# Attention and two expert layers on one core: the weights of the first layer converted in 16 pieces of 1024 columns instead of 32 of 512, with a new order of the first 32 steps

## The chip, the cores and the metric

The kernel runs on one core of a Trainium2 chip. A core has five engines with their own instruction queues, each worked off in order: PE (matrix products into PSUM), DVE (elementwise work and reductions), ACT (activation functions and copies), POOL (elementwise work on SBUF only, and indirect DMAs) and SP, which here issues the other DMAs. The metric is the device time of one execution in microseconds, as a median of runs.

## What is computed

```python
attn = chunked_attention(q, k, v)          # 8 batches, 8 heads, 576 tokens in chunks of 64, head_dim 64
x = attn as (4608 tokens, 512)
h = x @ w_in                               # (512, 2048)
g = max(h, 0) + alpha * min(h, 0)
x = g @ w_out                              # (2048, 512)
e = argmax(x @ w_gate)                     # 8 experts
out[token] = gate(token) * (max(x @ w1[e], 0) @ w2[e])
```

`w_in` and `w_out` come as float64; everything else is float32. Every product is made of three float32r products of a high and a low part of each operand (high x high, high x low, low x high).

## The kernel before

The tokens lie as 36 tiles of 128 rows in 18 batches j of two tiles. A *step* is one pair (j, m): `mm1` (X in the order below) makes 128 of the 2048 columns of h for a batch's 256 tokens, 12 matmuls of 256 columns; `mm2` (Y) multiplies them into the batch's two output tiles, 6 matmuls of 512 columns. There are 288 steps. Batches 0 and 1 are interleaved over the first 32 steps, group of columns by group (four groups g of 4 m): steps 0 to 3 are batch 0 with group 0, 4 to 7 batch 1 with group 0, 8 to 11 batch 0 with group 1, and so on. So group g's weights are wanted only from step 8 g on. From step 32 a loop runs over the steps; attention for later batches, gating, and the splitting of the expert weights (`eload`, `esplit`, written back to DRAM as `wsp`) are hung on step numbers. After step 287 come the experts, tile by tile, with their weights loaded into the same ring buffer (`load_early`, `refill`).

The first 32 steps are written out by hand as `ORDER`, a list of tokens, letter and number, worked off at build time; it sets the order within each engine's queue. The letters, with the line of the instruction in the profile:

- DMAs on SP: I piece of the weights (L481), Q and K q and k (L165, L167, L173, L174), V v (L178), N alpha.
- The conversion of piece k, from float64 words to a high and a low float32r part: v (ACT, L486) and s, u, m (DVE, L490, L495, L499) put together a float32 from the two 32-bit words; h (ACT, L502) rounds it to the high part; l (L506, on POOL with suffix G, on DVE with V) subtracts for the low part. v, s and u read the raw words, and the last of them frees their buffer.
- A step: X (PE, L331), r (ACT, L346) and x (DVE, L351, g_x in the code) apply alpha, f (ACT, L355) and g (L359, on POOL with G, on DVE with V; g_l in the code) split the result, Y (PE, L381). The PSUM banks for h alternate between two, and x is the last that reads one.
- Attention for tile i: S (PE, scores, L189), A, B (DVE, L202, L211), E (ACT, L218), C (DVE, three instructions, L223 to L225), D (L230, POOL or DVE), T (PE, L239), P (ACT, L245), O (PE, L302), H (ACT, L314) and L (DVE, L318) split it for mm1. A batch's X wants both its tiles' L.
- W warm-up matmuls (L914), p and b what else is hung on a step's number (gating from step 30, `load_wgb` and `fill_rows` at 24, the first `eload` at 25).

A piece is 128 rows by 512 columns of w_in (one quarter of the contracted dimension of a group) or 512 columns of w_out (one m). X of group 0 adds up over all four pieces 0 to 3; Y of m wants piece 4 + m. Raw words have four buffers (`sg_raw`), the float32 three (`sg_m`, later those of `eload` and of the expert rows `load`), u two (`sg_u`). The ring is two tiles; groups 0 and 2 lie in the first, 1 and 3 in the second:

```python
W_in = [ring[0][:, 0], ring[2][:, 0], ring[0][:, 1], ring[2][:, 1]]
W_out = [ring[1][:, 0], ring[3][:, 0], ring[1][:, 1], ring[3][:, 1]]
```

In the last 16 steps `load_early(0, c)`, c from 0 to 3, loads the first expert's weights over groups that are no longer needed, at steps 4, 7, 8 and 11 of the 16; `load_early(1, c)` follows in `START`, the written-out beginning of the experts' stage, where `m1` and `m2` are the two products.

Of the kernel before, what the change touches and what calls it, by code (L numbers as in the profile page):

```python
# [18 lines left out]
ORDER = """  # L19
I0 Q0 Q1 I1 N0 V0 I2 I3 Z0 W12 S0 S1 K1 s0V u0 A0 W10 B0 v0 E0 m0 I4 A1 C0 D0G s1V B1 T0 h0 E1 W6 v1 P0 u1 s2V C1 m1  # L20
I5 D1G l0G O0 T1 s3V u2 v2 P1 h1 l1G H0 v3 O1 S2 u3 m2 V1 I6 H1 h2 l2G S3 L0 m3 L1 A2 h3 v4 l3G I7 s4V B2 A3 E2 B3
p0 X0 r0 C2 x0 D2G b0 p1 E3 X1 f0 r1 v5 C3 u4 s5V m4 I8 x1 D3G g0G T2 v6 P2 h4 l4G b1 p2 X2 r2 T3 O2 u5 s6V m5 x2 u6
s7V I9 K2 P3 f1 h5 f2 m6 I10 b2 p3 g1V g2G l5G O3 X3 Y0 v7 H2 H3 h6 r3 v8 u7 L3 s8V x3 L2 u8 m7 I11 b3 p4 f3 h7 l6V
g3G s9V Y1 X4 r4 m8 x4 l7G b4 p5 h8 v9 X5 u9 I12 r5 f4 v10 l8G I13 s10V m9 x5 u10 s11V h9 u11 g4G m10 I14 V2 b5 Y2
p6 v11 f5 g5G l9G X6 r6 h10 l10G I15 m11 s12V x6 u12 s13V h11 v12 l11G m12 I16 b6 p7 Y3 X7 S4 r7 u13 x7 v13 h12 f6
l12G g6G I17 v14 s14V m13 u14 h13 l13G m14 I18 b7 Y4 p8 v15 f7 h14 g7G X8 Y5 s15V s16V u15 r8 l14G u16 x8 m15 I19 f8
v16 b8 p9 Y6 X9 r9 h15 A4 m16 g8G l15G I20 s17V v17 h16 l16G B4 u17 x9 I21 f9 b9 p10 g9G Y7 X10 r10 m17 s18V s19V
x10 u18 h17 E4 v18 v19 l17G b10 p11 f10 X11 r11 C4 I22 m18 u19 x11 D4G g10G v20 h18 l18G b11 S5 Y8 p12 f11 g11G Y9
X12 r12 s20V m19 I23 u20 x12 h19 l19G m20 I24 s21V f12 v21 h20 b12 p13 g12V l20G T4 X13 Y10 v22 P4 r13 u21 s22V u22
I25 m21 x13 h21 m22 I26 s23V u23 b13 p14 f13 g13G l21G X14 h22 r14 v23 s24V x14 l22G b14 Y11 p15 f14 g14G X15 Y12  # L30
r15 v24 u24 A5 x15 m23 I27 I28 v25 b15 p16 f15 h23 g15V l23G X16 Y13 r16 s25V m24 u25 B5 x16 v26 h24 f16 E5 b16 p17
g16G l24V X17 Y14 r17 s26V m25 x17 u26 C5 I29 f17 h25 s27V m26 I30 b17 p18 v27 l25G g17G X18 Y15 r18 x18 s28V u27
h26 v28 I31 b18 p19 f18 l26G g18G X19 Y16 r19 u28 m27 x19 v29 h27 b19 p20 f19 l27V D5V X20 v30 r20 s29V u29 m28 x20
m29 g19V s30V u30 b20 Y17 p21 h28 f20 l28G g20G Y18 X21 r21 h29 l29V x21 s31V m30 u31 b21 p22 f21 g21G X22 O4 T5 Y19
h30 r22 P5 v31 x22 m31 h31 f22 g22G l30V b22 p23 X23 r23 x23 b23 Y20 p24 f23 g23G l31G Y21 X24 r24 x24 b24 p25 f24 g24G
X25 Y22 r25 x25 b25 p26 f25 g25G X26 Y23 r26 x26 b26 Y24 p27 f26 X27 r27 x27 g26V b27 Y25 p28 f27 g27V X28 Y26 H4
r28 x28 b28 p29 f28 g28V X29 O5 r29 L4 x29 f29 H5 b29 Y27 p30 g29G X30 r30 L5 x30 b30 p31 Y28 X31 r31 f30 x31 b31
Y29 g30G
"""
# [3 lines left out]
def tile_attention_moe(ctx, tc, q, k, v, w_in, w_out, alpha, w_gate, w1, w2, out):  # L43
    nc = tc.nc
    NB = q.shape[0]
# [18 lines left out]

    duo = [ring_p.tile([128, 2, 2, 2, 4, 512], F32R, name=f"ring{c}") for c in range(2)]
    ring = [duo[c // 2][:, :, c % 2] for c in range(4)]
    W_in = [ring[0][:, 0], ring[2][:, 0], ring[0][:, 1], ring[2][:, 1]]
    W_out = [ring[1][:, 0], ring[3][:, 0], ring[1][:, 1], ring[3][:, 1]]

# [414 lines left out]
    def conv_v(k):
        im[k] = sg_m([128, 512], "m")
        nc.scalar.activation(out=im[k], in_=iraw[k][:, :, 1].bitcast(F32), func=ACTF.Abs, scale=2.0 ** -112)  # L486

    def conv_s(k, eng=nc.vector):
        iu[k] = sg_u([128, 512], "u", I32)
        eng.tensor_scalar(out=iu[k], in0=iraw[k][:, :, 0], scalar1=29, scalar2=None, op0=ALU.logical_shift_right)  # L490
# [535 lines left out]
```

## Time and profile before

| | us |
|---|---|
| median of 3 runs | 1364.6 (1363.75 to 1366.65) |
| the profiled execution | 1365.83 |
| its span, first to last instruction | 1364.1 |
| PE busy | 1319.9 (97%) |
| DVE busy | 998.6 (73%) |
| ACT busy | 740.8 (54%) |
| POOL busy | 725.1 (53%) |

Mean granted TensorE clock 0.99. PE is busy nearly throughout; in the page's 40 slices of 34 us its first four are at 7, 7, 8 and 8 tenths, and nearly all the others are full. DVE's first five are at 7, 9, 9, 6 and 6 tenths. The share over the whole span says little here, since the stages have different limits.

### The profile page before, as it was taken

To read this page: it belongs to the slowest core of one execution; us is meant where nothing else is said; L and a number is where in the kernel's file an instruction comes from. 1 tells how busy PE (TensorE), PEld (TensorE's weight loads), DVE (VectorE), ACT (ScalarE), POOL (GpSimd) and SP (SyncE) were. 2 spreads that over 40 slices of the span, in tenths; PEclk is the share of its full clock that TensorE was granted. 3 is DMA by queue.
4 is the path that set the end of the run, shared out by engine and by line. 5 is a ranking of instruction groups with operands and counts; after the bars stand their busy time and mean duration, and the time that the engine had idled before them with its cause. 6 is when DMAs were issued, how large, how long until landed. Compare 5 with 4: busy or idle time off the path is not lost. (4 is left out here: it accounts for less than half of the span.)

```text
span 1364.1 us, 29980 instructions
## 1 busy us (share of the span) xinstructions
PE 1319.9 (97%) x9515; PEld 1152.2 (84%) x9515; DVE 998.6 (73%) x2524; ACT 740.8 (54%) x1993; POOL 725.1 (53%) x754
## 2 busy tenths in 40 slices
PE   7788999999999999999999999999999999999997
PEld 6577899999999999999999999887788888888885
DVE  7996687788787878877877887558976556666553
ACT  4454544555555555555546455339666666656663
POOL 4563244676766656666665765343444444444442
PEclk9989999999999999999999999999999999999999
DMA  6655213666565666656666662194124526966660
GB/s 235 200 163 177 85 32 109 216 200 219 197 219 197 216 210 209 223 184 210 215 212 218 196 229 88 40 365 185 46 71 171 173 58 227 348 202 257 199 269 34
DMA packets 107105, 249.08 MB, mean 183 GB/s; under 512 B 15360, under 2 KB 36352, under 8 KB 102848
## 3 DMA queue, kind: packets, MB, share of 16 engines
q1 hardware_dynamic: 100944, 227.37, 49.7%
q0 software_dynamic: 6000, 19.70, 3.8%
q8 instruction: 84, 1.38, 0.4%
q14 instruction: 77, 0.63, 0.1%
HBM read 401.39 MB, written 88.91 MB: 359 GB/s over the span
## 5 line engine op out<-in xcount | busy, mean ns | idle before, releaser
L331 PEld LDWEIGHTS h<-xt,ring 128*128 128x128 f32 x3456 | 455.7, 193 | 44.2 <-DVE r L351 17.0
L331 PE MATMUL h<-xt,ring 128*128 128x256 f32 x3456 | 465.8, 285 | 16.8 <-DVE r L351 13.1
L381 PE MATMUL y<-ring,g 128*128 128x512 f32 x1728 | 453.7, 398 | 3.1 <-POOL g L359 2.1
L381 PEld LDWEIGHTS y<-ring,g 128*128 128x128 f32 x1728 | 306.3, 189 | 58.3 <-POOL g L359 3.0
L359 POOL TENSOR_TENSOR g<-r,g 128x256 fp32r<-128x256 f32 x281 | 237.6, 847 | 166.2 <-ACT g L355 146.0
L351 DVE SCALAR_TENSOR_TENSOR r<-r,calpha,h 128x256 f32<-128x256 f32 x288 | 137.0, 476 | 173.7 <-ACT r L346 173.1
L405 DVE CUSTOM_DVE_ANT_0 junk<-row,wgb 128x512 bf16<-128x512 f32 x288 | 257.5, 894 | 8.1 <-ACT row L393 3.8
L469 POOL TENSOR_TENSOR sp<-eraw,sp 128x512 fp32r<-128x512 f32 x128 | 179.3, 1401 | 107.0 <-ACT sp L468 99.1
L697 DVE TENSOR_SCALAR hx<-h 32x128 f32<-32x128 f32 x576 | 165.3, 287 | 89.9 <-PE h L679 82.4
L679 PE MATMUL y<-ring,hT 128*128 (+1 forms) x936 | 221.7, 392 | 4.8 <-POOL hT L667 2.6
L346 ACT ACTIVATE r<-h 128x256 f32<-128x256 f32 x288 | 110.1, 382 | 209.2 <-PE h L331 147.7
L679 PE MATMUL h<-ring,xT 128*128 (+1 forms) x936 | 219.1, 389 | 1.7 <-DMA ring<-wsp 1.7
L667 POOL TENSOR_TENSOR hT<-z,hT 128x512 fp32r<-128x512 f32 x78 | 100.7, 1309 | 220.7 <-ACT hT L666 219.5
L679 PEld LDWEIGHTS y<-ring,hT 128*128 128x128 f32 x936 | 176.1, 189 | 44.0 <-POOL hT L667 4.3
L679 PEld LDWEIGHTS h<-ring,xT 128*128 128x128 f32 x936 | 175.5, 188 | 38.4 <-issue 2.1
L355 ACT ACTIVATE g<-r 128x256 fp32r<-128x256 f32 x288 | 119.5, 415 | 147.6 <-PE y L381 106.3
L695 ACT ACTIVATE hx<-h 32x128 f32<-32x128 f32 x672 | 179.5, 267 | 10.3 <-PE h L679 2.8
L666 ACT ACTIVATE hT<-z 128x512 fp32r<-128x512 f32 x78 | 48.0, 633 | 115.4 <-DVE z L664 111.1
L260 ACT ACTIVATE px<-s 32x256 f32<-32x256 f32 x240 | 89.6, 374 | 3.1 <-DVE s L249 0.3
L468 ACT ACTIVATE sp<-eraw 128x512 fp32r<-128x512 f32 x128 | 80.5, 629 | 2.8 <-DMA wsp<-sp 2.1
L664 DVE STREAM_TRANSPOSE z<-xg 128x512 f32<-128x512 f32 x39 | 27.6, 707 | 47.5 <-POOL hT L667 47.4
L667 POOL TENSOR_TENSOR xT<-z,xT 128x512 fp32r<-128x512 f32 x39 | 51.7, 1326 | 16.1 <-ACT xT L666 15.5
(163 smaller groups left out, 958.3 us busy)
## 6 DMA issues: line engine op xcount, KB each, us to landing
ring<-wsp SPq DMA_DIRECT2D x70, 4096.0 KB
wsp<-sp SPq DMA_DIRECT2D x128, 512.0 KB
eraw<-in_w SPq DMA_DIRECT2D x128, 256.0 KB
ring<-wsp SPq DMA_DIRECT2D x8, 2048.0 KB
xg<-xs SPq DMA_DIRECT2D x156, 64.0 KB
vt<-in_v SPq DMA_DIRECT2D x18, 512.0 KB
qt<-in_q SPq DMA_DIRECT2D x17, 512.0 KB
kt<-in_k SPq DMA_DIRECT2D x17, 512.0 KB
```

The costliest lines, as they stand in the source:

```text
L331: nc.tensor.matmul(out=h, lhsT=w[:, wl, a, 128 * mi:128 * mi + 128], rhs=x[:, xl, a], start=(n == 0), stop=(n == 11),)
L346: nc.scalar.activation(out=r, in_=h, func=ACTF.Relu, scale=-1.0)
L351: nc.vector.scalar_tensor_tensor(out=r, in0=r, scalar=calpha[:, m:m + 1], in1=h, op0=ALU.mult, op1=ALU.add)
L355: nc.scalar.activation(out=gs[j, m][:, 0], in_=rs[j, m][0], func=ACTF.Copy)
L359: eng.tensor_tensor(out=g[:, 1], in0=r, in1=g[:, 0].bitcast(F32), op=ALU.subtract)
L381: nc.tensor.matmul(out=ys[j][t], lhsT=g[:, gl, 128 * t:128 * t + 128], rhs=w[:, wl, mi], start=(m == 0 and n == 0), stop=(m == MF - 1 and ...
L405: nc.vector.tensor_tensor_reduce(out=junk, in0=r[:, 0:512], in1=wgb[e // 2][:, e % 2], scale=1.0, scalar=0.0, op0=ALU.mult, op1=ALU.add, a ...
L469: eng.tensor_tensor(out=dst[:, 1], in0=raw, in1=dst[:, 0].bitcast(F32), op=ALU.subtract)
L667: nc.gpsimd.tensor_tensor(out=dst[:, 1], in0=z, in1=dst[:, 0].bitcast(F32), op=ALU.subtract)
L679: ins.append(nc.tensor.matmul(out=out, lhsT=lhs[:, xl, a], rhs=w[:, rows_, wl, a], start=(first and a == 0 and n == 0), stop=(last and a = ...
L695: nc.scalar.activation(out=dst, in_=src, func=ACTF.Relu)
L697: V.tensor_scalar(out=dst, in0=src, scalar1=0.0, scalar2=None, op0=ALU.max)
```

## The change

Each group now has four pieces: two of w_in, all four quarters of the contracted dimension for 256 columns (two m), and two of w_out, 512 columns for two m. So a piece is 1024 columns, its DMA 1 MB, and each of v, s, u, m, h, l handles 1024 columns in one instruction; X of m 0 and 1 wants piece 0 alone, X of m 2 and 3 piece 1, Y of m 0 and 1 piece 2. Groups 0 and 1 lie in the ring's first tile, 2 and 3 in the second. Until h of piece 8 is written, the second tile's memory is a buffer `stage` for the raw words of pieces 0 to 7; pieces 8 to 15 use two buffers of 8 KB a partition in turn, which later hold the gate's weights. u has one buffer (only DVE uses it), the float32 has two, r three. l runs on DVE but for pieces 0 and 2. `ORDER` is a new list with 51 warm-up matmuls instead of 28; it holds load_qk(3), load_v(3) (K3, V3) and the load of the gate's weights (G), which were hung on steps 20, 28 and 24; fill_rows and the first eload go from steps 24 and 25 to 31 and 32. `load_early(0, 2)` and `(0, 3)` go from steps 8 and 11 of the last 16 to 12 and 15.

The diff, its main parts; of the new order the beginning and the end:

```diff
+I0 Q1 N0 Q0 V0 I1 I2 Z0 W14 s0 v0 u0 W6 S1 m0 W2 S0 A1 h0 K1 I3 I4 I5 A0 l0G B1 B0 E1 E0 C1 C0 D1G v1 s1 D0V u1 W15 T0
+P0 m1 v2 W2 O0 T1 s2 H0 P1 L0 h1 W2 O1 u2 S2 V1 I6 I7 H1 l1V S3 K2 I8 I9 A2 m2 v3 B2 h2 A3 L1 E2 l2G B3 W10 X0 p0 C2
+E3 X1 p1 r0 C3 v4 D2G x0 b0 D3G r1 T2 s3 f0 X2 p2 P2 g0G x1 b1 T3 u3 f1 r2 X3 p3 g1G P3 x2 b2 m3 Y0 f2 r3 g2G x3 b3 O2
+h3 s4 Y1 H2 l3V f3 O3 g3G L2 v5 Y2 u4 H3 Y3 L3 m4 X4 p4 s5 h4 u5 S4 r4 X5 p5 x4 b4 m5 f4 X6 p6 r5 g4G x5 b5 h5 s6 Y4
+f5 l5V r6 g5G X7 p7 x6 b6 u6 f6 Y5 g6G r7 x7 b7 l4V f7 Y6 g7G A4 v6 X8 p8 B4 v7 m6 Y7 r8 s7 E4 X9 p9 h6 x8 b8 u7 f8 S5
+r9 l6V X10 p10 x9 b9 v8 m7 X11 p11 f9 r10 g8V g9G h7 x10 b10 Y8 s8 f10 r11 l7V X12 p12 x11 b11 v9 Y9 g10V u8 r12 f11
+X13 p13 g11G x12 b12 I10 m8 f12 Y10 g12G r13 x13 b13 h8 s9 X14 p14 f13 l8V g13G Y11 r14 x14 b14 u9 X15 p15 f14 v10
...
+x24 b24 m14 Y23 r25 f24 x25 b25 g24G h14 X26 p26 s15 f25 l14V X27 p27 r26 u15 Y24 r27 x26 b26 G0 g25V f26 X28 p28 m15
+g26G x27 b27 h15 Y25 C4 f27 r28 X29 p29 l15V g27G x28 b28 Y26 r29 D4V f28 g28G x29 b29 X30 A5 f29 g29G Y27 p30 r30 x30
+X31 p31 f30 g30G Y28 r31 x31 T4 Y29 B5 P4 E5 O4 C5 H4 D5V L4 T5 P5 O5 V3 H5 L5 b30 b31
...
+    duo = [ring_p.tile([128, 2, 2, 2, 4, 512], F32R, name="ring0")]
+    stage = shared_p.tile([128, 8, 2048], I32, tag="ring1", name="stage")
...
+    def second_half():
+        duo.append(shared_p.tile([128, 2, 2, 2, 4, 512], F32R, tag="ring1", name="ring1"))
+        use_ring(1)
...
+        for x in range(2):
+            y = slice(256 * x, 256 * x + 256)
+            ipieces.append((g, 0, y, w_in[g, :, :, y]))
+        for x in range(2):
+            y = slice(2 * x, 2 * x + 2)
+            ipieces.append((g, 1, y, w_out[g, :, y]))
+    spare = sg_raw([128, 2, 2048], "iraw", I32)
+    places = [stage[:, x] for x in range(8)] + 4 * [spare[:, x] for x in range(2)]
...
     def conv_h(k):
-        nc.scalar.activation(out=ipieces[k][0][:, 0], in_=im[k], func=ACTF.Copy)
+        if k >= 8 and len(duo) == 1:
+            second_half()
+        nc.scalar.activation(out=split(k)[0], in_=shaped(k, im[k]), func=ACTF.Copy)
...
-    at(24, load_wgb)
-    at(24, fill_rows)
+    at(31, fill_rows)
...
-    for c, d in ((0, 4), (1, 7), (2, 8), (3, 11)):
+    for c, d in ((0, 4), (1, 7), (2, 12), (3, 15)):
```

## Rows read from the trace of the kernel before

**Rows 1.** busy us (and instructions) of PE, PEld, DVE, ACT, POOL, then clock, DMA share, GB/s

```profile
0.00:10.00 10.00, 7.37 (x96) 7.03 (x97) 3.42 (x6) 2.85 (x4) 3.06 (x52) 1.00 0.78 254
5.00:124.00 119.00, 91.64 (x827) 78.17 (x827) 115.81 (x163) 61.13 (x126) 63.40 (x50) 0.93 0.59 198
...
150.00:200.00 50.00, 50.00 (x434) 45.14 (x433) 41.45 (x125) 25.40 (x70) 18.00 (x23) 1.00 0.14 42
```

**Rows 2.** timeline of PE: start, length, engine, line, what, count

```profile
22.02 1.64 PE L331 MATMUL h<-xt,ring 128*128 128x256 f32 x10 [2.28 <-DVE xt L318]
...
142.10 1.15 PE L302 MATMUL o<-pt,vt 64*64 64x64 f32 x32
...
146.19 0.69 PE L189 MATMUL s<-kt,qt 64*64 64x64 f32 x32
...
148.31 1.60 PE L331 MATMUL h<-xt,ring 128*128 128x256 f32 x12
149.74 1.55 PE L381 MATMUL y<-ring,g 128*128 128x512 f32 x6
151.13 3.04 PE L331 MATMUL h<-xt,ring 128*128 128x256 f32 x24
```

**Rows 3.** waits up to 151 us: total us, times, longest

```profile
PE h L331 <- DVE r L351: 13.1, 10, 3.0
```

**Rows 4.** timeline of DVE, undisturbed instructions

```profile
38.81 0.68 DVE L318 TENSOR_TENSOR xt<-o,xt 128x512 fp32r<-128x512 f32 x1
39.41 0.41 DVE L490 TENSOR_SCALAR u<-iraw 128x512 int32<-128x512 int32 x1
39.74 0.47 DVE L351 SCALAR_TENSOR_TENSOR r<-r,calpha,h 128x256 f32<-128x256 f32 x1
40.13 0.68 DVE L318 TENSOR_TENSOR xt<-o,xt 128x512 fp32r<-128x512 f32 x1
...
76.50 0.67 DVE L223 TENSOR_REDUCE sm<-p 128x8 f32<-128x512 f32 x1
...
77.54 0.64 DVE L499 SCALAR_TENSOR_TENSOR m<-m,u 128x512 int32<-128x512 int32 x1
```

**Rows 5.** groups by form, 5 to 127 us: count, busy us, mean ns, idle before

```profile
L499 DVE SCALAR_TENSOR_TENSOR m<-m,u 128x512 int32<-128x512 int32 x32 | 31.8, 997 | 0.6 <-ACT m L486 0.5
L495 DVE SCALAR_TENSOR_TENSOR u<-iraw,u 128x512 int32<-128x512 int32 x32 | 30.5, 960 | 0.2
L490 DVE TENSOR_SCALAR u<-iraw 128x512 int32<-128x512 int32 x32 | 26.7, 840 | 5.3 <-DMA iraw<-in_w_in 5.3
...
L359 POOL TENSOR_TENSOR g<-r,g 128x256 fp32r<-128x256 f32 x20 | 19.4, 969 | 20.3 <-ACT g L355 20.3
```

**Rows 6.** timelines of DVE and POOL around 29 us

```profile
28.96 1.27 DVE L490 TENSOR_SCALAR u<-iraw 128x512 int32<-128x512 int32 x1
...
28.66 1.29 POOL L230 TENSOR_TENSOR p<-p,sm 128x512 f32<-128x512 f32 x1 [0.43 <-ACT m L486]
```

**Rows 7.** instructions by source line, up to 140 us: least, median, longest ns

```profile
L506 POOL TENSOR_TENSOR ring<-m,ring x27: 1290/1485/1815, 15.9 to 126.5; 128x512 fp32r<-128x512 f32 x27
...
L359 POOL TENSOR_TENSOR g<-r,g x22: 735/914/1209, 29.9 to 131.4; 128x256 fp32r<-128x256 f32 x22
...
L502 ACT ACTIVATE ring<-m x32: 616/631/637, 9.7 to 123.4; 128x512 fp32r<-128x512 f32 x32
```

**Rows 8.** end of the steps: SP's ring loads, all DMAs of 890 to 935 us, PE

```profile
895.18 25.90 SPq L618 DMA_DIRECT2D ring<-wsp  x7
...
DMA packets 2035, 17.63 MB, mean 392 GB/s; under 512 B 366, under 2 KB 878, under 8 KB 1006
...
DMA  9699999899999999999999999899999998999952
...
933.12 0.73 PE L679 MATMUL y<-ring,hT 128*128 128x512 f32 x2 [1.39 <-ACT hT L666]
...
941.68 2.88 PE L679 MATMUL y<-ring,hT 128*128 128x512 f32 x12
```

More of the change, by code (lines that the diff above doesn't have):

```diff
@@ L25 @@
[L25 to L38, printed above, removed]
+I0 Q1 N0 Q0 V0 I1 I2 Z0 W14 s0 v0 u0 W6 S1 m0 W2 S0 A1 h0 K1 I3 I4 I5 A0 l0G B1 B0 E1 E0 C1 C0 D1G v1 s1 D0V u1 W15 T0
+P0 m1 v2 W2 O0 T1 s2 H0 P1 L0 h1 W2 O1 u2 S2 V1 I6 I7 H1 l1V S3 K2 I8 I9 A2 m2 v3 B2 h2 A3 L1 E2 l2G B3 W10 X0 p0 C2
@@ new lines @@
+g14V I11 Y12 r15 m9 s10 X16 p16 h9 x15 b15 u10 f15 Y13 r16 g15V I12 m10 X17 p17 l9V h10 Y14 r17 x16 b16 v11 l10V X18
+p18 f16 s11 Y15 r18 g16V v12 u11 Y16 x17 b17 I13 V2 m11 f17 X19 p19 g17V h11 s12 Y17 x18 b18 r19 l11V f18 X20 p20 g18G
+x19 b19 u12 f19 Y18 r20 g19G v13 x20 b20 I14 X21 p21 m12 f20 Y19 r21 g20V h12 x21 b21 s13 X22 p22 f21 l12V g21G Y20
+u13 r22 v14 X23 p23 x22 b22 I15 K3 m13 f22 Y21 r23 g22G x23 b23 h13 s14 X24 p24 f23 l13V Y22 r24 u14 X25 p25 g23V v15
+x24 b24 m14 Y23 r25 f24 x25 b25 g24G h14 X26 p26 s15 f25 l14V X27 p27 r26 u15 Y24 r27 x26 b26 G0 g25V f26 X28 p28 m15
@@ L63, in tile_attention_moe, with use_ring @@
     wsp = dram.tile([E, 4, 128, 2, 4, 512], F32R, name="wsp")
[L65 to L68, printed above, removed]
+    duo = [ring_p.tile([128, 2, 2, 2, 4, 512], F32R, name="ring0")]
+    stage = shared_p.tile([128, 8, 2048], I32, tag="ring1", name="stage")
+    W_in, W_out, W2 = [], [], []
+    def use_ring(c):
+        for h in range(2):
+            W_in.append(duo[c][:, h, 0])
+            W_out.append(duo[c][:, h, 1])
+            W2.append(duo[c][:, :, h])
+    def second_half():
+        duo.append(shared_p.tile([128, 2, 2, 2, 4, 512], F32R, tag="ring1", name="ring1"))
+        use_ring(1)
+    use_ring(0)
     ident = const.tile([128, 128], F32, name="ident")
@@ L114, in sg_raw, with sg_m @@
     def sg_raw(shape, name, dt=F32):
-        return sg_p.tile(shape, dt, tag="raw", name=name, bufs=4)
-    def sg_m(shape, name, dt=F32):
-        return sg_p.tile(shape, dt, tag="m", name=name, bufs=3)
+        return sg_p.tile(shape, dt, tag="raw", name=name, bufs=1)
+    trio = sg_p.tile([128, 3, 512], F32, name="trio")
+    trios = [0]
+    def sg_m():
+        trios[0] += 1
+        return trio[:, trios[0] % 3]
     def sg_u(shape, name, dt=F32):
@@ L169, in load_part_qk @@
     def load_part_qk(t):
-        if t == 0:
+        if 0 not in qs:
             qs[0] = qk_p.tile([128, 4, 256], F32, tag="qt", name="qt")
@@ new lines, in tile_attention_moe, with shaped, raw, split @@
+    spare = sg_raw([128, 2, 2048], "iraw", I32)
+    places = [stage[:, x] for x in range(8)] + 4 * [spare[:, x] for x in range(2)]
+    im = {}
+    iu = trio[:, 0:2].rearrange("p a f -> p (a f)").bitcast(I32)
+    def shaped(k, x):
+        return x.rearrange("p (a f) -> p a f", a=ipieces[k][3].shape[1])
+    def raw(k):
+        return places[k].rearrange("p (a f t) -> p a f t", a=ipieces[k][3].shape[1], t=2)
+    def split(k):
+        g, w, y, _ = ipieces[k]
+        w = (W_out if w else W_in)[g]
+        return [w[:, x, y] if ipieces[k][1] else w[:, x, :, y] for x in range(2)]
@@ L479, in iload @@
     def iload(k):
-        t = sg_raw([128, 512, 2], "iraw", I32)
-        nc.sync.dma_start(out=t.rearrange("p f t -> p (f t)"), in_=ipieces[k][1].bitcast(I32))
-        iraw.append(t)
+        nc.sync.dma_start(out=raw(k).rearrange("p a f t -> p a (f t)"), in_=ipieces[k][3].bitcast(I32))
     def conv_v(k):
[L485 to L490, printed above, removed]
+        im[k] = sg_u([128, 1024], "m")
@@ L492, in conv_u, with conv_s @@
+        nc.scalar.activation(out=shaped(k, im[k]), in_=raw(k)[:, :, :, 1].bitcast(F32), func=ACTF.Abs, scale=2.0 ** -112)
+    def conv_s(k):
+        nc.vector.tensor_scalar(
+            out=shaped(k, iu), in0=raw(k)[:, :, :, 0], scalar1=29, scalar2=None, op0=ALU.logical_shift_right,
+        )
     def conv_u(k):
-        t = iraw[k]
-        u = iu[k]
-        nc.vector.scalar_tensor_tensor(out=u, in0=t[:, :, 1], scalar=-(2 ** 31), in1=u, op0=ALU.bitwise_and, op1=ALU.bitwise_or)
+        u = shaped(k, iu)
+        nc.vector.scalar_tensor_tensor(
+            out=u, in0=raw(k)[:, :, :, 1], scalar=-(2 ** 31), in1=u, op0=ALU.bitwise_and, op1=ALU.bitwise_or,
+        )
@@ L545, in tile_attention_moe @@
             at(max(8 * (i - 2) - 5, 30) + d, f, i, *part)
-    for j in range(3, NB):
+    for j in range(4, NB):
         at(MF * (j - 2) + 4, load_qk, j)
@@ L574, in tile_attention_moe @@
         pre.setdefault(s0 + b, []).append((gate_b, (i,)))
-    at(24, load_wgb)
-    at(24, fill_rows)
+    at(31, fill_rows)
     for x in range(3):
-        at(25, eload)
+        at(32, eload)
     for x in range(len(epieces)):
         at(56 + 8 * x // 5, esplit)
-    W2 = [ring[c] for c in range(4)]
     cnt = {}
```

42 lines of the change are left out of this document (16 added, 26 removed).

## Prediction

> **What bounds the kernel now.** I read the busy time by windows first, then the waits, then the timelines of PE, DVE and POOL side by side. From about 150 us to the expert stage PE never pauses (the first of fourteen windows of 50 us, all full, stands in [rows 1]), so whatever the first 32 steps save or lose is passed on unchanged; nothing later has slack to swallow or return it, the expert stage's own pauses aside. The question is only when step 32 starts. In the trace that is 151.1 us [rows 2]. The first step starts at 22.0 us; 32 X, 30 Y and the attention work of tiles 2 to 5 fill some 96 of the 129 us between. The rest is PE waiting, most of it for DVE to finish g_x (L351) [rows 3], because a later X cannot have its PSUM bank before. DVE is the reason: from 5 to 124 us it is busy 115.8 of 119 us [rows 1].
>
> But DVE does not work all that time. Its own pace is seen where two instructions follow each other freely: 0.60 us for 512 columns, 0.33 for the shift, 0.39 for g_x [rows 4]. On that measure s should last about 0.4 us as written in the trace, u and m 0.69; their means are 0.84, 0.96 and 1.00 [rows 5]. The long ones lie under a POOL instruction: s at 28.96 lasts 1.27 us, to 30.23; the POOL multiplication that began at 28.66 ends at 29.95, and the 0.28 us behind it are the work of s itself [rows 6]. g_x, which reads one of its two inputs from PSUM, stays at 0.39.
>
> Own work of DVE up to 124 us: s 32 x 0.33, u and m 64 x 0.60, l 5 x 0.60, g_x 23 x 0.39, g_l 4 x 0.34, the softmax's A and B 12 x 0.60, C 6 x 1.04, D once and L four times 0.60: 10.6 + 38.4 + 3.0 + 9.0 + 1.4 + 7.2 + 6.2 + 3.0 = 78.8 us. So 115.8 - 78.8 = 37 us are holds. POOL's undisturbed work in that time is l 27 x 1.29, g_l 20 x 0.735 [rows 5, 7] and D, of l's shape, 5 x 1.29: 56 us. Each us of POOL arithmetic costs DVE 37 / 56 = 0.66 us.
>
> The Trainium skill ("SBUF — State Buffer", Who interferes with whom) has the same: a VectorE instruction with two SBUF inputs, or in a two-port mode, and a GpSimd instruction that reads SBUF exclude each other, and the second blocks until the first is done. The trace agrees with it. It also speaks against the change: it holds in both directions, so longer DVE instructions block POOL longer; by it POOL's g_l becomes the late one, which is the third rival below.
>
> **The change part by part.** *Pairs of pieces.* 32 conversions become 16 of 1024 columns. Of u's 0.60 us for 512 columns 0.06 are fixed, if s at 0.33 takes two columns where u takes one [rows 4]: 0.27 us per 256 columns. So s goes to 0.60, u, m and l to 1.13 us, and g_l, 256 columns, stands above at 0.34. No row shows these lengths. Their bounds without holds are 1.20, twice the present, and 1.08, nothing fixed left; I take 1.13, by the two lengths that are there. Fixed costs saved: 48 x 0.06 = 3 us. *l moves to DVE*: 14 of 16 there, two on POOL (2.4 us each by the slope from 0.735 for 256 to 1.29 for 512 columns). DVE own work up to l15V in the new order: s 16 x 0.60, u, m 32 x 1.13, l 14 x 1.13, g_x 28 x 0.39, g_l 9 x 0.34, A 5, B 5, L 4, D once at 0.60, C 5 x 1.04: 9.6 + 36.2 + 15.8 + 10.9 + 3.1 + 9.0 + 5.2 = 89.8 us, 11 more than before. POOL keeps l 4.8, D 3 x 1.29 and 17 g_l x 0.735 up to there: 21.2 us, which hold DVE 21.2 x 0.66 = 14.0. So the holds fall by 23 us, and the sum of both by 12.
>
> *Raw words in the ring's second half.* Ten pieces of 1 MB now have a place at once, where four of 512 KB had one. SP's queue no longer stands behind u for every piece from I4 on; in the new order only I10 to I15 wait for one. Each has the time from u(k-2) to s(k), at least 7 us of DVE work, for 1 MB. The ring's DMAs run at 392 GB/s [rows 8], those of the first 10 us at 254 [rows 1], so 2.7 to 4.1 us of transfer and one or two to start and land (I0, 0.5 MB and the program's first DMA, is waited for until 5.3 [rows 5]). That is hidden; without the cover each is 1 to 3 us, six times. *Finer order of need*: X0, X1 want only piece 0 and X2, X3 piece 1, so conversion l3 no longer stands ahead of X0; but S2, S3, s2, u2, m2 do now.
>
> *Start.* At the rate of 0 to 10 us [rows 1], I0's 1 MB is in at about 6.8 us (DVE starts at 5.3 now). DVE's list up to L1: s, u, m of 0 and 1 with s2, u2, m2 8.6, l1V 1.1, A and B of 0 and 1, A2, B2, A3 4.2, C 2.1, D0V 0.6, L0 and L1 1.2: 17.8 us. With 1.4 us for q and for the pass through O0 and H0, L1 ends at 26.0, against X0 at 22.0 now: 4 us later.
>
> *PE's route.* From X0: 32 X at 1.43 and 28 Y at 1.39 up to the end of X31 [rows 2] are 45.8 + 38.9; T2, T3, S4, S5 at 0.65 and O2, O3 at 1.15 [rows 2] 4.9. 26.0 + 89.6 = 115.6.
>
> *The end of the order.* Tile 5's softmax now hangs behind x31. From X31's end: r31, x31, B5 1.6; E5 stands on ACT behind P4, which wants Y28 and T4: 3.3; C5 4.4, D5V 5.1, T5 5.75, P5 6.4, O5 7.6, H5 8.2, L5 9.0 (ACT instructions at 0.6 [rows 7]). PE fills this with Y28, T4, Y29, O4, T5, O5, S6; 2.2 us stay open. In the trace there is no such gap [rows 2]. PE's route gives step 32 at 115.6 + 9.0 = 124.6.
>
> *DVE's route.* 6.8 + 89.8 + 14.0 and 3 us in which DVE has nothing: l15V at 113.6. Then Y26, X30, Y27, X31 5.6 and the 9.0: step 32 at 128.2.
>
> Two routes 4 us apart, on engines that wait for each other, do not simply give the later. Bounds for what they add: nothing, up to the 13 us that PE lost to g_x in the trace [rows 3], with DVE saturated. I take a quarter, 3.3: step 32 at 131.5, 19.6 us earlier.
>
> *Other moves, at nothing.* The gate's weights (G) go out after u15, their 2 MB at over 250 GB/s within 8 us; they are wanted at step 30, four steps of 2.8 us later. fill_rows and the first expert loads are 7 steps later in the order; their users come at steps 42 and 56. K3 and V3 are wanted at steps 30 and 38. 23 more warm-up matmuls run while PE has nothing else. A third r buffer can only free ACT.
>
> *The tail.* load_early(0, 2) and (0, 3) are four steps later, 11.3 us: their issues, now at about 896 and, three steps on, 904 [rows 8], become 907 and 915. The ring's 16.8 MB, under way now until about 933 [rows 8], then end at about 939: six of them, 12.6 MB, from 907 at 392 GB/s. m2(0, 0) begins at 933.1 and m2(0, 1) at 941.7 [rows 8]; the parts that they read land at about 913 and 920 in queue order, and at 939 at the latest if all share. Hidden by at least 2 us; uncovered it is 5.
>
> The profiled execution is 1365.8 us, 1.2 above the median of the runs. 1365.8 - 19.6 = 1346.2; as a median, **1345**.
>
> **The rivals.**
> 1. *The forecast*: step 32 between 126 and 137, 1340 to 1351. 0.55.
> 2. *Nothing added*: both engines mesh and L1 comes sooner; step 32 between 119 and 126, 1333 to 1340. For it: PE's route allows 124.6. Against it: DVE's route. 0.12.
> 3. *Longer instructions block*: POOL's g_l waits up to 1.1 us for each DVE instruction instead of 0.6, and g_x queues behind them. For it: POOL's 0.735 for g_l is already 0.97 in the mean [rows 7, 5]. If half of 22 g_l and 28 g_x are 0.4 us later on the path, 10 us go: 1355, between 1351 and 1361. 0.18. Late raw words (I10 to I15) would look alike in the time.
> 4. *The tail gives back*: the ring's last parts late for m2(0, 0) and m2(0, 1), 5 us, and the table's loads behind them as much: 1350 to 1356. 0.06.
> 5. *Slower*: the stretch belongs to DVE's own reading of these operands and not to POOL. Then s, u, m keep their means [rows 5], less the overlap of 0.09 each 2.53 us per 512 columns instead of 1.53: 81 us; l is of the same kind, 15.8 x 1.65 = 26; the other 28.2 stay. l15V comes at 6.8 + 135 + 3 = 145, step 32 14.6 later and with the 3.3 at 163: 12 us later than now, 1377. It decides where u, m and l of 1024 columns take over 1.7 us with POOL idle (1.13 x (1 + 33 / 61.6), 33 us being what fills DVE's route up to 151). Against it: the holds end with POOL's instructions [rows 6]. 0.05.
> 6. *No change*: the new waits for raw words and for POOL eat it all, 1362 to 1367. 0.04.
>
> Under 0.2% (2.7 us) a measurement of this kernel tells nothing. Faster: cases 1 to 4, 0.91; same 0.04; slower 0.05. The range 1337 to 1357 leaves out about half of 2, a fifth of 3, and 5 and 6: 0.19.
>
> **What would show it.** Right: u and m at 1.2 us nearly undisturbed, DVE's holds under 20 us; POOL's share in the first 130 us halved; X0 near 26; Y28 to Y29 and the step after them apart by some 2 us; step 32 at 127 to 137; PE without a pause afterwards; the ring's loads ending near 919, 939 less the 20 gained. Wrong: PE's waits for L351 as long as now; SP waiting for u with DVE idle behind s10 to s15; X0 after 30; m1 or m2 waiting for the ring.

## The result, and the profile after

The changed kernel takes 1345.51 us (median of 4 runs, 1344.22 to 1346.69) against 1365.62 before (four runs, one more than in the table of the kernel before), a ratio of 0.9853 [0.9836, 0.987]. The profiled execution takes 1346.69 us, 19.1 less than the one before.

Where the 19.1 us come from is read first: busy time by windows, the columns as in [rows 1].

```profile
5.00:124.00 119.00, 112.44 (x986) 102.54 (x986) 99.77 (x135) 64.71 (x110) 34.20 (x31) 0.96 0.54 201
...
150.00:200.00 50.00, 50.00 (x461) 45.02 (x461) 39.98 (x123) 22.95 (x64) 19.88 (x24) 1.00 0.17 48
```

In the first window PE has gained 20.8 us of work, DVE has fallen from 115.8 to 99.8 us and POOL from 63.4 to 34.2. From 150 us on PE is full, as before. The timeline of PE after, its start and the end of the written-out order, answers to [rows 2]:

```profile
22.28 1.10 PE L200 MATMUL s<-kt,qt 64*64 64x64 f32 x62
27.34 4.61 PE L940 MATMUL warm<-ident 128*128 128x128 f32 x20 [3.96 <-DVE xt L329]
31.60 3.88 PE L342 MATMUL h<-xt,ring 128*128 128x256 f32 x24
...
120.73 1.60 PE L342 MATMUL h<-xt,ring 128*128 128x256 f32 x12
122.16 1.55 PE L392 MATMUL y<-ring,g 128*128 128x512 f32 x6
...
127.48 0.66 PE L250 MATMUL t<-ident,p 128*128 128x128 f32 x4 [0.86 <-DVE p L241]
128.82 1.15 PE L313 MATMUL o<-pt,vt 64*64 64x64 f32 x32 [0.69 <-ACT pt L256]
131.39 0.69 PE L200 MATMUL s<-kt,qt 64*64 64x64 f32 x32 [1.42 <-DVE xt L329]
```

Step 32 (its X is the next instruction) starts at 132.02 us. Before it was 151.13: 19.1 us, the whole difference. So the 256 later steps and the experts' stage return nothing and add nothing. The first step starts 9.6 us later than before, at 31.60; from there to the end of X31 at 122.16 PE never waits. The waits up to 135 us, in the columns of [rows 3]:

```profile
DVE trio L514 <- DMA stage<-in_w_in: 6.4, 1, 6.4
...
PE warm L940 <- DVE xt L329: 4.0, 1, 4.0
...
PE t L250 <- DVE p L241: 3.2, 2, 2.3
...
PE s L200 <- DVE xt L329: 1.4, 1, 1.4
```

A row of PE waiting for g_x (r L362 now) no longer exists; it was 13.1 us [rows 3]. DVE waits for raw words once, for the very first. The conversion instructions by form, 5 to 117 us, DVE and then POOL, with the columns of [rows 5]:

```profile
L526 DVE SCALAR_TENSOR_TENSOR m<-m,trio 128x1024 int32<-128x1024 int32 x16 | 20.2, 1260 | 0.2
L535 DVE TENSOR_TENSOR ring<-m,ring 128x1024 fp32r<-128x1024 f32 x14 | 17.0, 1214 | 0.0
...
L520 DVE SCALAR_TENSOR_TENSOR trio<-stage,trio 128x1024 int32<-128x1024 int32 x8 | 10.8, 1352 | 0.1
L520 DVE SCALAR_TENSOR_TENSOR trio<-iraw,trio 128x1024 int32<-128x1024 int32 x8 | 10.3, 1284 | 0.0
L514 DVE TENSOR_SCALAR trio<-iraw 128x1024 int32<-128x1024 int32 x8 | 6.2, 772 | 0.0
...
L370 POOL TENSOR_TENSOR g<-r,g 128x256 fp32r<-128x256 f32 x19 | 23.2, 1224 | 60.7 <-ACT g L366 60.6
```

Twice the columns cost u only 1.35 us in its first eight pieces and 1.28 in the others, and m 1.26, where half of them had cost 0.96 and 1.00 [rows 5]. The price of 1.13 is met: u at 110.00, undisturbed, is followed at 111.13. POOL's g_l went the other way, from 0.97 to 1.22 us. The reason is seen where the two engines meet (timelines of DVE and of POOL, as [rows 6]):

```profile
36.34 1.78 DVE L520 SCALAR_TENSOR_TENSOR trio<-stage,trio 128x1024 int32<-128x1024 int32 x1
...
107.69 1.25 DVE L514 TENSOR_SCALAR trio<-iraw 128x1024 int32<-128x1024 int32 x1
108.86 1.21 DVE L535 TENSOR_TENSOR ring<-m,ring 128x1024 fp32r<-128x1024 f32 x1
110.00 1.21 DVE L520 SCALAR_TENSOR_TENSOR trio<-iraw,trio 128x1024 int32<-128x1024 int32 x1
111.13 0.47 DVE L362 SCALAR_TENSOR_TENSOR r<-r,calpha,h 128x256 f32<-128x256 f32 x1
```

```profile
36.29 2.42 POOL L370 TENSOR_TENSOR g<-r,g 128x256 fp32r<-128x256 f32 x2 [4.00 <-ACT g L366]
...
107.64 0.74 POOL L370 TENSOR_TENSOR g<-r,g 128x256 fp32r<-128x256 f32 x1 [5.60 <-ACT g L366]
```

At 107.64 POOL is first: its g_l takes 0.74 us and s, 0.69 us alone, takes 1.25. At 36.29 two g_l stand on POOL: the first holds u (1.78 us), u then holds the second, and the pair takes 2.42 instead of 1.47. The engine that comes second waits, on either side.

The end of the steps, in the rows that answer to [rows 8] (SP; the DMAs of 865 to 930 us, a digit for each 1.6 us; PE):

```profile
876.17 25.89 SPq L645 DMA_DIRECT2D ring<-wsp  x7
...
DMA  5257699999928599103799999999999999992003
...
914.11 0.74 PE L706 MATMUL y<-ring,hT 128*128 128x512 f32 x2 [1.39 <-ACT hT L693]
...
921.39 2.88 PE L706 MATMUL y<-ring,hT 128*128 128x512 f32 x12
```

m2(0, 0) begins 19.0 us earlier after the same wait of 1.39 us, m2(0, 1) 20.3 earlier. The DMAs rest for some 5 us from 891 us on, end near 924 (the forecast said 919), and no product waits for them.

### The profile page after: what moved, and what is told of

Its sections match the earlier page's. It is cut to its first block, busy times and chain, and to the rows that moved or that the text cites. A ratio compares the mean times of both kernels' runs of the same rounds, so it can differ in the third digit from the quotient of the medians.

```text
span 1344.7 us, 29901 instructions
## 1 busy us (share of the span) xinstructions
PE 1317.9 (98%) x9561; PEld 1155.1 (86%) x9561; DVE 980.0 (73%) x2489; ACT 738.2 (55%) x1961; POOL 690.1 (51%) x725
## 5 line engine op out<-in xcount | busy, mean ns | idle before, releaser
L342 PE MATMUL h<-xt,ring 128*128 128x256 f32 x3456 | 459.9, 283 | 0.0
L370 POOL TENSOR_TENSOR g<-r,g 128x256 fp32r<-128x256 f32 x279 | 241.1, 865 | 201.7 <-ACT g L366 199.1
L362 DVE SCALAR_TENSOR_TENSOR r<-r,calpha,h 128x256 f32<-128x256 f32 x288 | 137.2, 476 | 171.4 <-ACT r L357 170.7
L480 POOL TENSOR_TENSOR sp<-trio,sp 128x512 fp32r<-128x512 f32 x128 | 179.5, 1402 | 106.2 <-ACT sp L479 99.4
L479 ACT ACTIVATE sp<-trio 128x512 fp32r<-128x512 f32 x128 | 80.5, 629 | 1.1 <-DMA wsp<-sp 0.5
L691 DVE STREAM_TRANSPOSE z<-trio 128x512 f32<-128x512 f32 x39 | 27.6, 707 | 47.4 <-POOL hT L694 47.4
```

Source lines behind the costliest of these rows:

```text
L342: nc.tensor.matmul(out=h, lhsT=w[:, wl, a, 128 * mi:128 * mi + 128], rhs=x[:, xl, a], start=(n == 0), stop=(n == 11),)
L362: nc.vector.scalar_tensor_tensor(out=r, in0=r, scalar=calpha[:, m:m + 1], in1=h, op0=ALU.mult, op1=ALU.add)
L370: eng.tensor_tensor(out=g[:, 1], in0=r, in1=g[:, 0].bitcast(F32), op=ALU.subtract)
L480: eng.tensor_tensor(out=dst[:, 1], in0=raw, in1=dst[:, 0].bitcast(F32), op=ALU.subtract)
```

## The experiments

All have 4 runs. "Less" is the median less that of the kernel before on the same chip; "step 32" is its start in the profiled execution. Up to L1 the change and kernels 1, 2, 7, 8, 9 and 10 have the same order, and yet L1 starts at 25.0 to 26.6 us in their traces, and what is behind it moves along; so step 32 is read with the waits beside it.

| kernel | median, us | less | ratio | step 32 |
|---|---|---|---|---|
| the change | 1345.51 | 20.1 | 0.9853 [0.9836, 0.987] | 132.0 |
| 1 without W10 | 1342.95 | 23.6 | 0.9827 [0.981, 0.9843] | 128.5 |
| 2 warm-up in bank h1 | 1341.41 | 25.1 | 0.9816 [0.9797, 0.9834] | 127.2 |
| 3 every l on POOL | 1354.37 | 12.1 | 0.9915 [0.9898, 0.9932] | 140.2 |
| 4 before, every l on DVE | 1355.78 | 10.7 | 0.9925 [0.9908, 0.9941] | 141.8 |
| 5 halves | 1346.56 | 19.5 | 0.9855 [0.9839, 0.9871] | 132.0 |
| 6 two places | 1344.61 | 21.5 | 0.9847 [0.9831, 0.9864] | 130.3 |
| 7 order of need undone | 1348.53 | 17.8 | 0.9872 [0.9855, 0.9888] | 132.5 |
| 8 end rewritten | 1344.28 | 21.8 | 0.9841 [0.9824, 0.9857] | 129.2 |
| 9 = 2 with 8 | 1341.45 | 24.6 | 0.982 [0.9803, 0.9836] | 127.3 |
| 10 = 2, another end | 1339.79 | 25.9 | 0.9815 [0.9798, 0.9831] | 124.7 |
| 11 = 10, L1 early | 1340.63 | 25.0 | 0.982 [0.9803, 0.9837] | 126.5 |
| 12 order alone | 1350.01 | 15.7 | 0.9881 [0.9865, 0.9898] | 136.1 |

**Who makes DVE slow: l on POOL, or DVE's own operands?** Kernel 3 gives every l of the changed kernel to POOL; kernel 4 gives every l of the kernel before to DVE and changes nothing else.

```diff
-... l1V ... l3V ... l15V ...
+... l1G ... l3G ... l15G ...
```

> The changed kernel with all sixteen l on POOL. Theory (POOL's instructions hold DVE's, 0.66 us for each us): DVE's own work falls by 15.8 us, but POOL's grows by 33.6 us, so holds by 22; the means of u and m rise from 1.3 us to 1.6 or more, DVE's busy time up to 114 us from 95 to about 100, and with l at 2.4 us apiece and late behind g_l step 32 comes 4 to 15 us later: 1349 to 1360. Rival (the stretch belongs to DVE's operands): u and m stay at 1.22 to 1.3, DVE's busy time falls to about 80 us, and the time stays at 1345 or gains.

```diff
-... l0G ... l1G ... l31G ...
+... l0V ... l1V ... l31V ...
```

> The kernel before, its order kept, with all 32 l on DVE (27 of them were on POOL). Theory (holds): DVE gets 27 x 0.60 = 16 us of own work, POOL loses 35 us and with it 23 us of holds; the sum falls by 7 us, the means of s, u, m fall to about 0.5, 0.75, 0.75 us, and step 32 comes 4 to 9 us earlier: 1356 to 1361. Rival one (operands): DVE's list grows by 16 to 27 us: 1380 or more. Rival two (the new order is all): no gain in an order made for l on POOL, 1363 to 1368.

Groups by form, 5 to 124 us, of kernel 3:

```profile
L535 POOL TENSOR_TENSOR ring<-m,ring 128x1024 fp32r<-128x1024 f32 x16 | 39.7, 2481 | 28.8 <-ACT ring L531 27.3 <-PE h L342 1.5
...
L526 DVE SCALAR_TENSOR_TENSOR m<-m,trio 128x1024 int32<-128x1024 int32 x16 | 23.7, 1479 | 0.4 <-ACT m L511 0.2
L520 DVE SCALAR_TENSOR_TENSOR trio<-iraw,trio 128x1024 int32<-128x1024 int32 x8 | 19.1, 2388 | 0.1
...
L520 DVE SCALAR_TENSOR_TENSOR trio<-stage,trio 128x1024 int32<-128x1024 int32 x8 | 11.9, 1493 | 0.1
```

and of kernel 4, with its busy time (columns as in [rows 1]) and PE's wait for g_x:

```profile
L499 DVE SCALAR_TENSOR_TENSOR m<-m,u 128x512 int32<-128x512 int32 x32 | 24.3, 759 | 0.5 <-ACT m L486 0.5
L495 DVE SCALAR_TENSOR_TENSOR u<-iraw,u 128x512 int32<-128x512 int32 x32 | 24.2, 757 | 0.2
...
L490 DVE TENSOR_SCALAR u<-iraw 128x512 int32<-128x512 int32 x32 | 14.8, 466 | 5.0 <-DMA iraw<-in_w_in 5.0
...
5.00:124.00 119.00, 96.52 (x883) 84.44 (x882) 106.60 (x194) 64.52 (x133) 34.24 (x32) 0.96 0.65 215
...
PE h L331 <- DVE r L351: 8.0, 6, 2.9
```

The same u on the same operands takes 1.28 us with l on DVE and 2.39 with l on POOL in the later eight pieces (1.35 and 1.49 in the first eight; m 1.26 and 1.48), and the old m, u and s fall from 1.00, 0.96 and 0.84 us [rows 5] to 0.76, 0.76 and 0.47 when nothing but l moves. The stretch belongs to POOL's instructions. Both times go the way of the theory, kernel 3's within what was expected, kernel 4's 0.2 us below it. Two signs expected of kernel 3 did not come: m stays under 1.6 us, and DVE's busy time up to 114 us is 91.8 instead of 100; DVE has not come as far with its list there (105 instructions; 126 in the change, 13 of them l). Kernel 4 gets 10.7 us, about half of the change's 20.1, though DVE has taken over 27 instructions: its busy time to 124 us falls from 115.8 [rows 1] to 106.6. In that kernel PE still waits 8.0 us, six times, for g_x. Seen from the changed kernel, l on DVE is worth 8.0 us (20.1 less 12.1, kernel 3).

**The width of the instructions.** Kernel 5 keeps pieces, places and order, and issues s, u, m and l in two halves of 512 columns:

```diff
-        nc.vector.scalar_tensor_tensor(out=m, in0=m, scalar=3, in1=iu, ...)
+        for x in (slice(0, 512), slice(512, 1024)):
+            nc.vector.scalar_tensor_tensor(out=m[:, x], in0=m[:, x], scalar=3, in1=iu[:, x], ...)
```

> The changed kernel with each DVE instruction of the conversion (s, u, m and l) issued as two of 512 columns; loads, ACT's instructions and the order stay. Theory (what gained is that POOL no longer holds DVE, and DVE now has time over): some 62 more DVE instructions at 0.06 us, 4 us, vanish in the 14 us in which DVE has nothing up to 114 us; PE still does not wait between X0 and X31 and the time stays within 1.5 us of 1345.5. Rival (the length of the instructions made the gain): 4 us or more come back, 1349 or more.

1.05 us above the change, under what the runs tell apart. DVE is busy 106.4 us to 124 us instead of 99.8, more than the 4 us of fixed cost that were expected, but PE waits only 0.2 us more for it. POOL's g_l comes down to 0.98 us beside the shorter instructions, and no gain shows; PE waits for a g_l in neither kernel, so its lateness in the changed one is not on the path.

**The places for raw words.** Kernel 6 has no `stage`; all pieces use the two spare buffers in turn, and each I stands behind the last reader of the piece two before it.

```diff
-    places = [stage[:, x] for x in range(8)] + 4 * [spare[:, x] for x in range(2)]
+    places = 8 * [spare[:, x] for x in range(2)]
```

> The changed kernel without the waiting room in the ring's second half: all sixteen pieces pass through the two buffers that pieces 8 to 15 had, and I(k+2) stands in the order right behind the last reader of piece k. Theory: each load still has 7 us of DVE work or more before its s, and 1 MB lands in 4 to 5 us, so nothing waits: within 1.5 us of 1345.5. Rival (the raw words' room made the gain): loads come 1 to 3 us late, DVE waits for DMAs, 1350 to 1370.

Not slower (step 32 is earlier because the start was, see the last section). SP stands behind u for 77.6 us in sum, and DVE still waits for a DMA only once, at the start. The eight places in the ring's second half hide nothing that was not hidden.

**The order of need.** Kernel 7 cuts w_in by quarters of the contracted dimension again, so that every X of a group needs both its pieces, and moves l9 and l13 ahead of the X that then needs them.

```diff
-            y = slice(256 * x, 256 * x + 256)
-            ipieces.append((g, 0, y, w_in[g, :, :, y]))
+            y = slice(2 * x, 2 * x + 2)
+            ipieces.append((g, 0, y, w_in[g, :, y]))
...
-... s10 X16 ... l9V ...      -... X24 ... l13V ...
+... s10 ... l9V X16 ...      +... l13V X24 ...
```

> The changed kernel with a piece of w_in again one half of the contracted dimension for all 512 columns, so that X of m 0 to 3 wants both pieces of its group; l9V and l13V stand ahead of X16 and X24 for it. Width, waiting room and the rest of the order stay as changed. Theory: what came back with all novelties undone is X16's wait for piece 9 (its second six matmuls stood 0.75 and 1.28 us for the high and the low part there), and this cut alone shows the same wait: step 32 about 2 us later, 1347 to 1348.5. Rival: that wait needs the halves too (DVE's list longer by 4 us), and nothing shows here: 1345 to 1346.

Waits of PE in kernel 7, 24 to 137 us:

```profile
PE h L342 <- DVE ring L535: 2.2, 2, 1.8
```

X16 and X24 wait 2.2 us for l9 and l13. From its start to the next instruction's X16 takes 3.58 us and X24 2.08, where an X takes 1.43: 2.8 us more. The median is 3.0 us above the change (2.3 by the differences to before), at the limit of what the runs tell, but the waits are seen: the finer order is worth 2 to 3 us. Step 32 comes only 0.5 us later because L1 started 1.5 us sooner and the warm-up with X0 and X1 took 1.2 us less (last section).

**What is left to the order.** Kernel 12 puts 5, 6 and 7 together: halves, two places, quarters. What it keeps of the change is the new order with l on DVE, loads of 1 MB, ACT's instructions of 1024 columns and the groups' places in the ring.

> The changed kernel with all of its pieces' novelties undone at once, its order kept: DVE's conversion instructions in halves of 512 columns, all raw words through two buffers, and a piece of w_in again one half of the contracted dimension for all 512 columns, so that X of m 0 to 3 wants two pieces (two l are moved a few places up for it, ahead of X16 and X24). What stays of the change is l on DVE and the new order. Theory (l's engine and the order are the gain): within 3 us of 1345.5. Rival (width, room and finer need gain together what none gains alone): 1350 or more, and PE waits for l or for g_x.

It is 4.5 us above the change, not within the 3 that were expected; 1350 is where the rival stood, and PE does wait. X16 takes 4.22 us here and X24 2.06, so 3.4 of the 4.1 us that step 32 is late stand where kernel 7 lost 2.8. It gains 15.7 us, of which kernel 4 shows 10.7 to be l's. What is left, 5 us, is put down to the written order; no run has the new order with l on POOL and the old pieces, so this is a remainder and not shown by itself. Width, places and order of need together bring 4.4, most of which is kernel 7's.

**The late start.** The changed kernel's W10 stands behind L1. The warm-up writes PSUM bank h0, which O1 wrote and L1 reads, so it can't begin before L1 is done. Kernel 1 drops it; kernel 2 puts 15 warm-up matmuls into the other bank.

```diff
-... l2G B3 W10 X0 ...
+... l2G B3 X0 ...
```

> The changed kernel without the ten warm-up matmuls (W10) ahead of X0. In its trace they wait for L1 until 27.3 us, since they write the PSUM bank that L1 reads, and then run for 4.3 us at half clock, so that X0 starts at 31.6 us. Theory: PE's work from X0 on sets the end (PE does not wait once between X0 and X31), so X0 moves to 27.3, X0 and X1 take over the stretch at half clock (about 1.5 us of the gain lost), and step 32 comes 2.5 to 4 us earlier: 1341.5 to 1343. Rival: DVE's route binds right behind PE's; then PE waits for g_x instead and step 32 stays within 1 us: 1345.

```diff
-        def warm(n):
-            b = bank("h0", "warm")
+        def warm(n, tag="h0"):
+            b = bank(tag, "warm")
...
-... l2G B3 W10 X0 ...
+... l2G B3 M15 X0 ...          # M: warm(n, "h1")
```

> The changed kernel with fifteen warm-up matmuls in place of those ten, into the bank that X0 takes next and that nobody reads at that time. They need not wait for L1, so they run from S3's end at 23.4 us to about 27.2, and X0 starts at 27.3 at full clock. Theory (PE's route sets the end): step 32 4.5 to 5.5 us earlier, 1340 to 1341.5. Rival (DVE's route right behind): within 1 us, 1345.

The start in the timelines of PE, kernel 1 and then kernel 2:

```profile
27.02 4.31 PE L342 MATMUL h<-xt,ring 128*128 128x256 f32 x23 [3.02 <-DVE xt L329]
```

```profile
23.61 3.62 PE L940 MATMUL warm<-ident 128*128 128x128 f32 x30
27.37 3.12 PE L342 MATMUL h<-xt,ring 128*128 128x256 f32 x24
```

Kernel 1 starts X0 as soon as L1 is done, and runs X0 and X1 at the lower clock in 4.31 us (3.12 at full clock). Kernel 2 has the warm-up ended and the clock up when L1 ends: 4.1 us faster than the change in the median (5.0 by the differences to before), 4.8 in step 32. Both times are as expected.

**The end of the order.** Kernels 8 and 9 move T4 ahead of X31 and pull the softmax of tile 5 forward; kernel 10 moves T4 ahead of X30, T5 ahead of Y28 and O5 ahead of Y29.

```diff
-X30 A5 f29 g29G Y27 p30 r30 x30 X31 p31 f30 g30G Y28 r31 x31 T4 Y29 B5 P4 E5 O4 C5 H4 D5V L4 T5 P5 O5 V3 H5 L5
+X30 A5 f29 g29G Y27 T4 p30 r30 x30 P4 B5 X31 p31 E5 f30 g30G O4 C5 Y28 D5V r31 x31 T5 H4 L4 Y29 P5 O5 V3 H5 L5
```

> The changed kernel with the end of its order rewritten: T4, P4, B5, E5, O4, C5 and D5V, which stood behind X31, Y28 and x31, are moved up between Y27 and Y28, so that tile 5's softmax runs beside X31 and Y28. Nothing else changes. Theory (PE's route sets the end and the 3.0 us of waiting for D5V, P5 and L5 at its end are on it): PE waits 0.8 us there instead of 3.0, 2.2 us less: 1343 to 1344. Rival (x30, x31 or a PSUM bank is late for it): the wait moves to X31 or T4 and the time stays within 1 us.

> The changed kernel with both: warm-up matmuls ahead of X0 in the other bank, and the rewritten end. Theory: PE's route sets the end from L1 on, so both gains add, 4.5 + 2.2 us: step 32 near 125.3 us, 1338 to 1340. Rival: with X0 4 us sooner DVE's route (l14V and l15V) is the later one at the end, and Y24 or Y26 waits: 1341 to 1343.

```diff
-X30 A5 f29 g29G Y27 p30 r30 x30 X31 p31 f30 g30G Y28 r31 x31 T4 Y29 B5 P4 E5 O4 C5 H4 D5V L4 T5 P5 O5 V3 H5 L5
+T4 X30 P4 A5 f29 g29G B5 Y27 p30 r30 E5 x30 C5 X31 p31 f30 g30G O4 D5V T5 H4 L4 P5 Y28 r31 x31 O5 Y29 V3 H5 L5
```

> The warm-up matmuls in the other bank, and a second rewriting of the end: T4 before X30, so that it doesn't take the bank that X31 wants, T5 before Y28, O5 before Y29, and Y29 behind it as cover for H5 and L5. Theory: X31 no longer waits for x30 (1.0 us in the first rewriting), and of the 1.4 us for L5 (the next scores, S6, use the bank that L5 reads, so they can't cover it) all but 0.2 us go under Y29: step 32 at about 124.7 us, 3 us earlier than with the warm-up edit alone: 1338 to 1339. Rival: a PSUM bank or the single p buffer makes T4, O4 or T5 wait instead: 1341.

Timelines of PE, kernel 9 and then kernel 10:

```profile
117.99 1.69 PE L342 MATMUL h<-xt,ring 128*128 128x256 f32 x12 [1.04 <-DVE r L362]
...
126.69 0.69 PE L200 MATMUL s<-kt,qt 64*64 64x64 f32 x32 [1.43 <-DVE xt L329]
```

```profile
119.42 0.66 PE L250 MATMUL t<-ident,p 128*128 128x128 f32 x4 [1.21 <-DVE p L241]
...
124.07 0.69 PE L200 MATMUL s<-kt,qt 64*64 64x64 f32 x32
124.69 3.12 PE L342 MATMUL h<-xt,ring 128*128 128x256 f32 x24
```

The first rewrite missed. T4 takes the turn of the bank that X31 would have had, so X31 waits 1.04 us for x30, as the rival of kernel 8 had it; and, which neither side had named, S6 writes the bank that L5 reads, so it waits as before. 2.46 us of waits replace 2.97, and kernel 9 equals kernel 2, where 1338 to 1340 were expected. Kernel 8's step 32 is 2.8 us earlier than the change's mostly for its start: L1 comes 1.1 us sooner, and the warm-up with X0 and X1 takes 1.35 us less. The second rewrite leaves one wait of 1.21 us at the end. Its median is 1.6 us below kernel 2's, 0.8 by the differences to before: the waits are seen to go, but the size is under what the runs tell apart, and the 1338 to 1339 expected are not reached. It is the fastest kernel of the study.

**An earlier L1.** Kernel 11 takes kernel 10 and moves L1, and with it X0, ahead of A2, B2, A3 and B3, x0 and x1 ahead of C2 and C3, and X2 ahead of T2.

```diff
-... I8 I9 A2 m2 v3 B2 h2 A3 L1 E2 l2G B3 M15 X0 p0 C2 E3 X1 p1 r0 ...
+... I8 I9 L1 M4 X0 p0 A2 m2 v3 B2 h2 A3 r0 E2 l2G X1 p1 B3 x0 b0 ...
```

> The same, and L1 moved ahead of A2, m2, B2 and A3 on DVE, with x0 and x1 ahead of C2 and C3 and X2 ahead of T2, so that X0 starts near 24.3 us instead of 27.3. Theory: DVE's work ahead of X4 (l3V, L2, L3) is ready by 39 us, before PE needs it, so about 2 of the 3 us stay: 1336 to 1337.5. Rival: DVE's route ahead of X2 to X4 is the limit there, PE waits between X1 and X4 and nothing is gained.

Waits of PE in kernel 11, 24 to 130 us:

```profile
PE t L250 <- POOL p L241: 2.3, 2, 1.2
PE t L250 <- DVE p L241: 1.7, 1, 1.7
```

X0 starts at 24.93 us, 1.0 earlier than in kernel 10, and T2 and T3 wait 2.3 us for the softmax that was pushed back; S4 comes 1.3 us later, at 44.36 instead of 43.04. The 1336 to 1337.5 expected are missed, and nothing is gained, as the rival had it. The waits suggest that the start is bound by the list ahead of S4 as a whole and not by where L1 stands in it.

## Why the prediction was right, and where its terms were off

1345 us were forecast and 1345.5 measured; step 32 at 131.5, and at 132.0 in the trace. The mechanism of the gain held: l on DVE takes away most of the holds, and what the first 32 steps save is kept to the end. What it said of the engine that ends last did not hold, and the close agreement is luck. Along PE the forecast reads 26.0 to X0, 89.6 for the steps, 9.0 for the end, and 6.9 us that DVE adds (3.6 because its route was the later one, 3.3 of interplay). The trace has 31.6, 90.6, 9.9, and nothing that DVE adds. A start 5.6 us late stands where 6.9 us of DVE were expected, and one of the signs that were to show the forecast wrong, X0 after 30, did come.

- **Right: POOL's l holds DVE, and l on DVE is cheaper than l on POOL.** Kernels 3 and 4 show it from both sides and refute rival 5, whose mark for u was 1.7 us with POOL idle; undisturbed it is 1.21. The 1.13 us of u, m and l from start to start were measured as 1.13, the 2.4 of POOL's l as 2.39.
- **Holds of 14.0 us: mis-sized.** DVE is busy 96.6 us from its start to the end of l15V at 115.6 (the window below); less its own 89.8 that leaves 6.8 us at most. Another part of the price fell on POOL: its 19 g_l took 1.22 us instead of 0.735 [rows 7], 9.3 us more. The forecast's 14.0 was of DVE alone. Its 0.66 us of DVE per us of POOL was read where POOL ran long l's; with short g_l among DVE instructions of 1.2 us POOL waits more than DVE. The Trainium skill ("SBUF — State Buffer", Who interferes with whom) says that the order of issue decides who waits; the two pairs of instructions above agree.

The changed kernel from DVE's first instruction to the end of l15V, columns as in [rows 1]:

```profile
6.37:115.60 109.23, 102.67 (x925) 93.60 (x924) 96.58 (x130) 61.44 (x102) 30.74 (x25) 0.95 0.55 206
```

- **Rival 3 had its mechanism right and its price wrong.** POOL's g_l became longer, as it said: 1.22 us against 0.97 before and 0.735 undisturbed. But POOL idled 60.6 us for ACT in front of those g_l and had room, and g_x, which reads h from PSUM, was not queued behind it: the mean of its 29 is 0.476 us. Kernel 5 shortens g_l to 0.98 us and gains nothing, and PE waits for no g_l.
- **"23 more warm-up matmuls run while PE has nothing else", costed at nothing: the step that failed.** L1 ended at 27.2 us, 1.2 later than forecast. Then W10 still had to run, and PE, idle for 3.96 us before it, ran it at half clock: 4.26 us. X0 came at 31.6 instead of 26.0. Kernel 2 gets 4.1 us back. The cover that I named, an idle PE, was gone once W10 had to wait for the same L1 as X0.
- **DVE's route as the later one, and 3.3 us of interplay: neither was there.** X0 to the end of X31 took 90.6 us, forecast 89.6 for PE alone, and PE never waited. The late start had let DVE run ahead: in its idle time stand 3.80 us before the first g_x, and 12.7 us in all to l15V (the same window) where 3 were forecast. But an early X0 does not bring DVE's route back: in kernel 2, with X0 at 27.4, PE never waits between X0 and X31 either. In kernel 10, whose end is another, X0 comes at 25.95, where the forecast had it, PE waits for no g_x, and step 32 starts at 124.7; PE's route alone had given 124.6. DVE's route was over-sized, its holds being 7 us less.
- **The end: 3.0 us open, 2.2 forecast.** Right in kind (T5, O5 and S6 wait for tile 5's softmax); S6 can't fill the gap, since its bank is the one that O5 and L5 use.
- **Places and tail at nothing: right.** Kernel 6, and the rows of the tail. Finer order of need, which had no term of its own, is 2 to 3 us.

By parts, from kernels 4, 12 and the change: l on DVE 10.7 us, the order 5.0 as a remainder, and order of need with wide instructions and places 4.4; 4 more lay in the bank of the warm-up and about 1 in the end. The first is known to some 2 us, the half-width of an interval, the others, differences of two such, to some 3; and taken off in another sequence the parts differ, as the 8.0 us for l by kernel 3 show. Rival 2's 1333 to 1340 was reached by kernel 10 at 1339.8, with the start and the end mended.

## What to carry to other kernels

Where DVE (VectorE) and POOL (GpSimd) both work on SBUF at once, moving POOL's long instructions to DVE can make DVE's total time fall, as it did in kernel 4 (115.8 to 106.6 us): compare each instruction's mean with its undisturbed length before calling an engine full. Where the two hold each other up, ask which engine comes second, and whether that one has slack. A filler that "runs while the engine is idle" is free only if what it writes has been free for long: ask of each which buffer it takes, and who reads that last.
